# Where the zero fill of the output stands in the queue: a pooled attention with a noisy top-2 mixture of experts

## The chip, the cores and the metric

The kernel runs on one core of a Trainium2 chip. The metric is the device time of one execution in microseconds (us); lower is better. The engines that matter here are TensorE (PE in the profile, with PEld for its weight loads), VectorE (DVE), ScalarE (ACT), GpSimd (POOL), and SyncE (SP), which in this kernel does nothing but issue DMA transfers. DMA transfers issued by SP go through one hardware queue, those issued by POOL through one software queue.

## What is computed

Inputs are q, k and v of shape 8 x 8 x 576 x 64 (batch, heads, positions, head size). Keys and values are averaged over groups of 8 positions, so each query looks at 72 pooled keys. The attention result, rearranged to 4608 tokens of 512 numbers, goes into a mixture of 8 experts; each token takes its two best experts by noisy logits.

```
k_p, v_p = k.reshape(B,H,S/8,8,D).mean(3), v.reshape(B,H,S/8,8,D).mean(3)
attn = softmax(scale * q @ k_p^T) @ v_p                # 4608 tokens x 512
noisy = x @ w_gate + log1p(exp(x @ w_noise)) * noise
top2  = the two largest of noisy; weights = softmax over the two
out = zeros(4608, 512)
for e in 8 experts:  for both ranks k:
    rows = tokens whose rank-k expert is e
    out[rows] += weight * (relu(x[rows] @ w1[e]) @ w2[e])
```

w1 is 512 x 1024 and w2 is 1024 x 512 per expert. The output must start from zeros because rows are added to it expert by expert.

## The kernel before

**First part, attention (up to about 187 us of the profile).** The batch is taken in four pairs (`pr` 0 to 3), each pair in nine chunks of 128 tokens (`ci` 0 to 8), 36 chunks in all (27 to 35 are the last pair). A chunk consists of score matmuls (line 379 or 372), softmax exponentials on ACT (line 386), transposes of the exponentials (line 403) that ACT copies out of PSUM (tile `eT`, line 405), the value matmuls (line 416), and normalisation on DVE (line 427, tile `xr`). Finished tokens are written to the scratch tensor `x_dram` (line 437), by POOL in pairs 0 to 2 and by SP in the last pair. Queries of a later unit are transposed into `qp` (line 353) and copied by ACT to `qT` (line 355).

**Routing.** After each pair, `route` computes the two experts of its tokens and their places; 18 indirect DMAs per pair (line 614, POOL) scatter (token, weight) records to `rec_dram`. Two early reads of the records (tile `raw`, line 645, POOL) fetch expert 0's first lists: after the records of pair 1, and after those of pair 2. POOL then turns them into row numbers (line 684) and gathers the tokens (tile `xg`, line 706).

**Second part, the experts (from about 187 us).** The work is a list of 24 groups, three per expert; for expert 0 the groups have tiles 0 to 3, 4 to 6 and 7 to 9. `split` transposes the gathered tokens (line 928, tile `xp`) and splits them in a high and a low part (`xh`, `xl`, line 939); `stage1` multiplies by w1 in eight blocks `f` (line 968; PSUM tile `ph` with three buffers, emptied by ACT line 973 and DVE line 974); `stage2` multiplies by w2 (line 1072) and `finish` scatters results to the output (line 1014). Tiles 0 to 3 of expert 0 hold tokens of the output's lower half alone.

**Weights.** Each expert's weights come in eight loads of 512 KB through a staging tile `wst` with three buffers (line 463, SP) and are cast by ACT (line 484, high part) and DVE (line 485, low part). Expert 0's first three w1 loads are issued by SP when pair 3 begins, and the casts stand in ACT's and DVE's program at chunks 30 to 32.

**The zero fill.** `zt` is a cleared tile. `zero()` (line 124) writes it to 384 rows of the output (768 KB, line 128, SP); twelve of them cover the 4608 rows. `ZP` says after which chunk how many are emitted, and `issue_after` tells the scheduler behind which instruction they may stand in the order. The first six are the lower half, the last six the upper half (group `zero1`).

**Order.** A scheduler orders each engine's instructions when the program is built; on the chip each engine runs its own list strictly in that order and waits at semaphores.

Of the kernel before, what the change touches and what calls it, by code (L numbers as in the profile page):

```python
# [20 lines left out]
def kernel(  # L21
# [12 lines left out]
    nc = tc.nc  # L34
    B, H, S, D = q.shape
    NTOK, DM = out.shape
    E = moe_w_gate.shape[1]
    DF = moe_w1.shape[2]
    P = 128
# [7 lines left out]
    NP = B // 2  # L47
# [68 lines left out]
    ps2.tile([P, 512], F32, tag="s", name="s_first", bufs=2)  # L116

    ZW = 3
    ZP = {23: (21, 21, 22, 22), 24: (23, 23), 25: (24, 24), 26: (25, 25), 27: (26, 26)}
    lastx, laste, lastt = [None], [None], [None]  # L120
    zt = ap_.tile([P, DM], F32, name="zt")
    zn = [0]

    def zero(ins):
        i = zn[0]
        zn[0] += 1
        with tc.issue_after(ins):
            z = nc.sync.dma_start(out[i * ZW * P:(i + 1) * ZW * P, :].rearrange("(p r) m -> p r m", p=P),
                                  zt.unsqueeze(1).to_broadcast([P, ZW, DM]))
        if i * ZW * P >= XT0:  # L130
            tc.add_to_no_dep_group("zero1", z.ins)

# [207 lines left out]
    def qtr(u, half, hp=None):  # L340
        kind, pr, b, jp = u
        if half == 0:
            QTT[u] = ap_.tile([P, H, P], F32, tag="qT", name=f"qT{pr}_{b}_{jp}", bufs=2)
        elif kind == "R":
            return
        qT = QTT[u]
        qp = ps2.tile([P, 4, P], F32, tag="one", name=f"qp{pr}_{b}_{jp}_{half}", bufs=2)
        for i in range(4):
            if kind == "R":
                src = QR[pr][:, 2 * i:2 * i + 2]  # L350
            else:
                src = QT[b][:, half * 4 + i, 2 * jp:2 * jp + 2]
            nc.tensor.transpose(qp[:, i], src.rearrange("p a d -> p (a d)"), ident)
        with tc.high_priority(offset=HP if hp is None else hp):
            nc.scalar.copy(qT[:, half * 4:half * 4 + 4], qp)
# [94 lines left out]
    WST, wld = {}, {}  # L450
    genl = [None]

    def wload(e, i, h):
        st = wp.tile([P, DF], F32, tag="wst", name=f"wst{e}_{i}_{h}", bufs=WS)
        if i < 2:
            src = moe_w1[e].rearrange("(p c) f -> p c f", p=P)[:, 2 * i + h]
            dst = st
        else:
            r0 = (i - 2) * 4 * P + h * 2 * P
            src = moe_w2[e, r0:r0 + 2 * P, :].rearrange("(c p) f -> p c f", p=P)  # L460
            dst = st.rearrange("p (c f) -> p c f", c=2)
        with tc.issue_after(genl[0]) if (e, i, h) == (1, 2, 0) else nullcontext():
            wld[e, i, h] = nc.sync.dma_start(dst, src).ins
        WST[e, i, h] = st
# [27 lines left out]
    def drain(g):  # L492
        for _ in g:
            pass
# [227 lines left out]
    def fetch(g):  # L722
        e, t0, nt = g
        for t in range(t0, t0 + nt):
            gather(e, t)
# [12 lines left out]
    lgs = {}  # L738
    gens = []

    def advance(n, m):
        for _ in range(n):
            while gens:
                try:
                    next(gens[0])
                    break
                except StopIteration:
                    gens.pop(0)
        for _ in range(min(m, len(scq))):
            scq.pop(0)()  # L750
# [52 lines left out]
    for b in range(2, B):  # L803
        c = 9 * ((b - 2) // 2) + (0 if b % 2 == 0 else 4)
# [7 lines left out]
    for b in range(1, B):  # L812
        c = 9 * (b // 2) + (0 if b % 2 == 0 else 4)
# [29 lines left out]
    for i, (ui, u, jj) in enumerate(chunks):  # L843
# [17 lines left out]
        for o in order + ("" if "b" in order else "b") + ("" if "x" in order else "x"):  # L861
# [14 lines left out]
            elif ui + 2 < NU:  # L876
                qtr(units[ui + 2], "qr".index(o))
        for j in ZP.get(i, ()):
            zero(lx[j])
# [204 lines left out]
    def wadvance(n):  # L1084
        for _ in range(n):
            while wgens:
                try:
                    next(wgens[0])
                    break
                except StopIteration:  # L1090
                    wgens.pop(0)
# [3 lines left out]
    s0 = SP_[0]  # L1095
    fetch(groups[1])
    rt = route(NP - 1, 0, NCH, lgs[NP - 1], mone)

    def hook0(f):
        with tc.issue_after(s0[0].ins), tc.issue_after(s0[1].ins):  # L1100
            if f < 2:
                next(rt, None)
                next(rt, None)
            elif f == 2:
                next(rt, None)
            elif f == 5:
                drain(rt)
                advance(0, 100)
            if f < 4:
                with tc.issue_after(evict[0].ins), tc.issue_after(evict[1].ins):  # L1110
                    wadvance(2)
        if f == 4:
            for i, h in ((0, 0), (0, 1), (1, 0)):
                with tc.issue_after(wld[0, 3, 1]):
                    wload(1, i, h)
# [23 lines left out]
    for i, g in enumerate(groups):  # L1139
        e = g[0]  # L1140
        if i % NG == 1 and e + 1 < E:
            wgens += [weights(e + 1, 0), weights(e + 1, 1)]
        stage1(g, (hook0, hook2)[i] if i < 2 else None)
        if i:
            if i == 2:
                with tc.issue_after(hli[g, 2].ins):
                    split(groups[i + 1])
            elif i > 2 and i + 1 < len(groups):
                split(groups[i + 1])
            if i % NG != 1:  # L1150
                wadvance(100)
        if i % NG == NG - 1 and e + 1 < E:
            wgens += [weights(e + 1, 2), weights(e + 1, 3)]
        stage2(g, (lambda: fetch(groups[i + 2])) if 1 < i < len(groups) - 2 else (lambda: None),
               hook if i == 0 else hook1 if i == 1 else hookw if i % NG == NG - 1 else None)
        if i == 1:
            fetch(groups[3])
        if i == 0:
            lates.append(load_recs(0, E, 0, 4))
            fetch(groups[2])  # L1160
            with tc.issue_after(hli[g, NFB - 1].ins):
                wadvance(100)
# [113 lines left out]
```

## Time and profile before

| | us |
|---|---|
| median of 3 timed runs | 1045.96 (1044.1 to 1049.59) |
| span of the profiled execution, first to last instruction | 1040.8 |
| median of the timed runs minus that span | 5.16 |
| PE busy in the span | 1011.7 (97%) |
| DVE / ACT / POOL busy | 561.2 / 339.5 / 636.6 |

The profile gives the profiled execution's time as its span alone; the last line but two is what lies around it if that execution was like the median run. Times in the rows below count from the first instruction of the span. "Busy" leaves out waits and the issuing of DMAs; a row of the timeline shows in brackets how long the engine stood idle before it and what ended the wait.

### The profile page before, as it was taken

What the parts mean: (1) busy time and instruction counts of PE and PEld (TensorE: products, weight loads), DVE (VectorE), ACT (ScalarE), POOL (GpSimd) and SP (SyncE); (2) the same over time, 40 slices, a digit from 0 to 9 for tenths busy, and PEclk for the clock granted to TensorE, in tenths of its full rate; (3) what the DMA queues carried; (4) which work ended last, traced back from release to release, by engine and by line L of the source; (5) the groups of instructions that cost most, each with busy time, mean ns of one, the idle gap of its engine ahead of it and who ended that gap; (6) DMA issues with size and microseconds to landing.
All of it is one profiled execution on the core that took longest, in us unless ns stands there. A gap on an engine that the chain in (4) does not pass through costs nothing. (4 is left out here: it accounts for less than half of the span.)

```text
span 1040.8 us, 16075 instructions
## 1 busy us (share of the span) xinstructions
PE 1011.7 (97%) x5896; PEld 913.7 (88%) x5896; DVE 561.2 (54%) x1288; ACT 339.5 (33%) x857; POOL 636.6 (61%) x662
## 2 busy tenths in 40 slices
PE   7999996999999999999999999999999999999997
PEld 6999895789998998899889988998899889988995
DVE  6899884833464545444644464446445544564331
ACT  5778885512222222122222222222222222222110
POOL 4005373573776777767767776777577756773541
PEclk9999998999999999999999999999999999999998
DMA  9998996614234423442344234424432443232200
GB/s 330 365 345 246 300 314 191 160 48 115 91 91 132 140 64 104 138 134 69 117 129 140 66 113 129 130 79 118 120 124 86 114 122 117 82 91 87 69 20 32
DMA packets 77028, 142.13 MB, mean 137 GB/s; under 512 B 24501, under 2 KB 32778, under 8 KB 76948
## 3 DMA queue, kind: packets, MB, share of 16 engines
q1 hardware_dynamic: 48628, 78.33, 24.8%
q0 software_dynamic: 28320, 62.77, 19.9%
q8 instruction: 47, 0.77, 0.3%
q14 instruction: 33, 0.27, 0.1%
HBM read 103.78 MB, written 39.17 MB: 137 GB/s over the span
## 5 line engine op out<-in xcount | busy, mean ns | idle before, releaser
L968 PE MATMUL ph<-xh,w 128*128 128x384 f32 (+2 forms) x1536 | 403.9, 344 | 0.7 <-ACT xh L939 0.7
L714 POOL DMA_INDIRECT xg<-x_dram,x x266 | 261.4, 983 | 91.7 <-issue 68.3
L968 PEld LDWEIGHTS ph<-xh,w 128*128 128x128 f32 x1536 | 274.5, 188 | 21.1 <-ACT xh L939 0.9
L973 ACT ACTIVATE hh<-ph 128x512 fp32r<-128x512 f32 (+2 forms) x192 | 97.8, 509 | 548.5 <-PE ph L968 547.8
L1072 PE MATMUL py<-w,hh 128*128 128x512 f32 x896 | 276.5, 390 | 0.0
L968 PE MATMUL ph<-xl,w 128*128 128x320 f32 (+2 forms) x768 | 263.7, 344 | 0.0
L974 DVE SCALAR_TENSOR_TENSOR hl<-ph,hh 128x512 fp32r<-128x512 f32 (+2 forms) x192 | 111.3, 580 | 221.2 <-ACT hh L973 221.1
L1072 PEld LDWEIGHTS py<-w,hh 128*128 128x128 f32 x896 | 167.7, 188 | 34.3
L1072 PE MATMUL py<-w,hl 128*128 128x512 f32 x448 | 174.5, 390 | 0.0
L968 PEld LDWEIGHTS ph<-xl,w 128*128 128x128 f32 x768 | 144.2, 188 | 10.3
L1010 DVE SCALAR_TENSOR_TENSOR pv<-py,raw,pv 128x128 f32<-128x128 f32 x196 | 54.9, 342 | 130.9 <-PE py L1072 125.7
L1043 PE MATMUL py<-hh,w 128*128 128x320 f32 x512 | 112.8, 309 | 0.0
L1057 POOL DMA_INDIRECT out_dram<-pv,o x80 | 84.8, 1060 | 36.1 <-issue 13.7
L1072 PEld LDWEIGHTS py<-w,hl 128*128 128x128 f32 x448 | 84.1, 188 | 17.6
L1031 POOL DMA_INDIRECT pv<-out_dram,o x70 | 72.9, 1041 | 37.8 <-DMA out_dram<-pv,raw 18.6
L1014 POOL DMA_INDIRECT out_dram<-pv,raw x56 | 59.7, 1066 | 59.1 <-DVE pv L1010 32.0
L614 POOL DMA_INDIRECT rec_dram<-rec,pos x72 | 74.8, 1039 | 30.0 <-issue 20.1
L485 DVE TENSOR_TENSOR w<-wst,w 128x512 fp32r<-128x512 f32 x128 | 87.6, 688 | 9.7 <-ACT w L484 9.1
L1043 PEld LDWEIGHTS py<-hh,w 128*128 128x128 f32 x512 | 85.6, 188 | 0.0
L484 ACT CAST w<-wst 128x512 fp32r<-128x512 f32 x128 | 77.3, 615 | 15.2 <-DMA wst<-in_moe_w_dram 12.3
L1043 PE MATMUL py<-hl,w 128*128 128x320 f32 x256 | 79.1, 309 | 0.0
L934 DVE STREAM_TRANSPOSE xt<-xg 128x512 f32<-128x512 f32 (+1 forms) x70 | 70.9, 1035 | 3.2 <-DMA xg<-x_dram,x 2.2
(157 smaller groups left out, 982.4 us busy)
## 6 DMA issues: line engine op xcount, KB each, us to landing
wst<-in_moe_w_dram SPq DMA_DIRECT2D x64, 512.0 KB, 3.6
v<-in_v_dram SPq DMA_DIRECT2D x23, 512.0 KB, 9.2
out_dram<-zt SPq DMA_DIRECT2D x12, 768.0 KB, 19.7
k<-in_k_dram SPq DMA_DIRECT2D x7, 1280.0 KB, 11.6
q<-in_q_dram SPq DMA_DIRECT2D x7, 1024.0 KB, 12.9
x_dram<-xr POOLq DMA_DIRECT2D x12, 512.0 KB, 8.1
xg<-x_dram,x POOLq DMA_INDIRECT x276, 2.6
x_dram<-xr SPq DMA_DIRECT2D x4, 512.0 KB, 14.0
```

The lines of the kernel that those rows point to most:

```text
L484: nc.scalar.copy(hv, sv)
L485: nc.vector.tensor_sub(lv, sv, hv.bitcast(F32))
L614: s = nc.gpsimd.indirect_dma_start(out=rec_dram[:, :], out_offset=bass.IndirectOffsetOnAxis(ap=pos[:, i, c:c + 1], axis=0), in_=rec[:, c, ...
L714: nc.gpsimd.indirect_dma_start(out=xg[:, r * P:(r + 1) * P], out_offset=None, in_=x4, in_offset=bass.IndirectOffsetOnAxis(ap=xi[e, t][:, r ...
L934: nc.vector.transpose(xt[:, :nr], xg[:, :nr * P].rearrange("p (r i b) -> p r b i", i=32, b=NDB))
L968: nc.tensor.matmul(ph[:, :n], w1s(e, a, db, f), xs[b][:, db, :n], start=(i == 0), stop=(i == 3 * NDB - 1))
L973: ra = nc.scalar.activation(hh[:, :n], ph[:, :n], AF.Relu)
L974: rd = hli[grp, f] = nc.vector.scalar_tensor_tensor(hl[:, :n], ph[:, :n], 0.0, hh[:, :n].bitcast(F32), op0=OP.max, op1=OP.subtract)
L1031: g = nc.gpsimd.indirect_dma_start(out=pv4[:, i], out_offset=None, in_=out4, in_offset=bass.IndirectOffsetOnAxis(ap=oi4[e, t0 + i // 4][:, ...
L1043: nc.tensor.matmul(py[:, :n], w2s(e, b, f)[:, mb * P:(mb + 1) * P], hs[f][a][:, :n], start=(i == 0), stop=(i == 3 * NFB - 1))
L1057: s = nc.gpsimd.indirect_dma_start(out=out4, out_offset=bass.IndirectOffsetOnAxis(ap=oi4[e, t0 + i // 4][:, i % 4], axis=0), in_=r4[:, i], ...
L1072: lastm[0] = nc.tensor.matmul(py, hs[f][a][:, cs], w2s(e, b, f), start=(i == 0), stop=(i == 3 * NFB - 1))
```

## The change

The twelve zero transfers are placed otherwise. The lower six stay with `zt` as their source and move from chunks 23 to 27 to chunks 28 to 33, one each. The upper six move to the second part: they are emitted at block `f == 4` of the first group's `stage1`, to stand behind expert 0's last w2 load (`wld[0, 3, 1]`) and ahead of expert 1's first three w1 loads. Their source is no longer `zt`, whose memory is given to other tiles by then, but the logits tile of the last pair, whose first 512 columns are cleared by a new DVE memset at block `f == 2`.

```
-    ZP = {23: (21, 21, 22, 22), 24: (23, 23), 25: (24, 24), 26: (25, 25), 27: (26, 26)}
+    ZP = {28: (27,), 29: (28,), 30: (29,), 31: (30,), 32: (31,), 33: (32,)}
...
-    def zero(ins):
+    def zero(ins, src=None):
...
-                                  zt.unsqueeze(1).to_broadcast([P, ZW, DM]))
+                                  (zt if src is None else src).unsqueeze(1).to_broadcast([P, ZW, DM]))
...
     rt = route(NP - 1, 0, NCH, lgs[NP - 1], mone)
+    zrow = lgs[NP - 1].rearrange("p n h c -> p (n h c)")[:, :DM]
...
     def hook0(f):
...
+        if f == 2:
+            nc.vector.memset(zrow, 0.0)
         if f == 4:
+            while zn[0] * ZW * P < NTOK:
+                zero(wld[0, 3, 1], zrow)
             for i, h in ((0, 0), (0, 1), (1, 0)):
                 with tc.issue_after(wld[0, 3, 1]):
                     wload(1, i, h)
```

SP's list in the last quarter of the attention, before: `zt` rows are zero transfers, `wst_0_0`, `wst_0_1` and `wst_1_0` are expert 0's first three w1 loads (512 KB each), `q` the last query load, `xr` rows the tokens of pair 3.

```order
L274 DMA qr_1550<-in_q_dram 64x8x64
L128 DMA out_dram<-zt 384x1x512 x4
L269 DMA q_1899<-in_q_dram 128x8x256
L128 DMA out_dram<-zt 384x1x512 x8
L463 DMA wst_0_0_2195<-in_moe_w_dram 128x1024
L463 DMA wst_0_1_2197<-in_moe_w_dram 128x1024
L463 DMA wst_1_0_2199<-in_moe_w_dram 128x1024
L437 DMA x_dram<-xr_6_0_0_2166 128x1024
```

The same place of SP's list in the changed kernel:

```order
L274 DMA qr_1550<-in_q_dram 64x8x64
L463 DMA wst_0_0_2183<-in_moe_w_dram 128x1024
L463 DMA wst_0_1_2185<-in_moe_w_dram 128x1024
L463 DMA wst_1_0_2187<-in_moe_w_dram 128x1024
L128 DMA out_dram<-zt 384x1x512 x2
L269 DMA q_1899<-in_q_dram 128x8x256
L128 DMA out_dram<-zt 384x1x512 x4
L437 DMA x_dram<-xr_6_0_0_2156 128x1024
```

The three w1 loads have moved from behind twelve zero transfers to ahead of all; six zero transfers are left, two ahead of the query load and four behind it.

SP's list where the second part begins, before: `wst_3_0` and `wst_3_1` are expert 0's last two w2 loads, the later `wst_0_0`, `wst_0_1` and `wst_1_0` expert 1's first w1 loads.

```order
L463 DMA wst_3_0_2838<-in_moe_w_dram 128x2x512
L437 DMA x_dram<-xr_7_1_0_2638 128x1024
L463 DMA wst_3_1_2861<-in_moe_w_dram 128x2x512
L463 DMA wst_0_0_2884<-in_moe_w_dram 128x1024
L463 DMA wst_0_1_2886<-in_moe_w_dram 128x1024
L463 DMA wst_1_0_2888<-in_moe_w_dram 128x1024
```

The same place in the changed kernel:

```order
L463 DMA wst_3_0_2832<-in_moe_w_dram 128x2x512
L437 DMA x_dram<-xr_7_1_0_2632 128x1024
L463 DMA wst_3_1_2856<-in_moe_w_dram 128x2x512
L128 DMA out_dram<-lg_2110 384x1x512 x6
L463 DMA wst_0_0_2885<-in_moe_w_dram 128x1024
L463 DMA wst_0_1_2887<-in_moe_w_dram 128x1024
L463 DMA wst_1_0_2889<-in_moe_w_dram 128x1024
```

Six zero transfers with the cleared logits as their source now stand between expert 0's last load and expert 1's first.

## Rows read from the trace of the kernel before

**Rows 1.** The page: span of the profiled execution.
```profile
span 1040.8 us, 16075 instructions
```
**Rows 2.** Windows: stretch, length, busy us (instructions) per engine, PE clock, DMA share, GB/s.
```profile
165.00:170.00 5.00, 1.68 (x8) 1.57 (x8) 2.40 (x5) 2.43 (x5) 0.58 (x1) 0.50 0.29 88
...
190.00:1000.00 810.00, 809.97 (x4299) 729.75 (x4300) 398.23 (x823) 197.24 (x385) 548.64 (x545) 1.00 0.35 105
```
**Rows 3.** Timeline, 166 to 173 us: start, duration, engine, line, what, [idle before <-releaser].
```profile
166.37 1.14 ACT L484 CAST w<-wst 128x512 fp32r<-128x512 f32 x2 [11.28 <-DMA wst<-in_moe_w_dram]
...
168.32 1.97 PE L353 MATMUL qp<-ident,q 128*128 128x128 f32 x8 [9.36 <-ACT eT L405]
...
172.61 0.43 PE L403 MATMUL ep<-ident,ex 128*112 128x128 f32 x2
```
**Rows 4.** Timeline of SP's DMA issues: start, time to issue them.
```profile
104.28 6.56 SPq L128 DMA_DIRECT2D out_dram<-zt  x4
...
119.27 27.33 SPq L128 DMA_DIRECT2D out_dram<-zt  x8
146.65 6.64 SPq L463 DMA_DIRECT2D wst<-in_moe_w_dram  x3
...
198.13 8.32 SPq L463 DMA_DIRECT2D wst<-in_moe_w_dram  x4
```
**Rows 5.** Tile `wst`, loads issued from 146 to 158 us.
```profile
DMA to landing us min/median/max: 16.8/18.3/19.7
```
**Rows 6.** Timeline of PE, the same kind of chunk one pair earlier.
```profile
117.78 1.04 PE L353 MATMUL qp<-ident,q 128*128 128x128 f32 x8
...
120.28 0.32 PE L403 MATMUL ep<-ident,ex 128*112 128x128 f32 x1
```
**Rows 7.** Tile `zt`: its memset (ns min/median/max), and its twelve transfers.
```profile
L185 POOL MEMSET zt<- x1: 565/565/565, 8.8 to 8.8; 128x512 f32 x1
...
DMA to landing us min/median/max: 13.8/19.7/21.7
```
**Rows 8.** Timeline of POOL: records, the two early reads, gathers.
```profile
155.53 1.02 POOL L614 DMA_INDIRECT rec_dram<-rec,pos  x1 [0.30 <-issue]
165.60 0.58 POOL L645 DMA_DIRECT2D raw<-rec_dram  x1 [9.04 <-DMA rec_dram<-rec,pos]
...
175.02 0.95 POOL L706 DMA_INDIRECT xg<-x_dram,x  x1 [0.31 <-issue]
...
198.65 0.97 POOL L614 DMA_INDIRECT rec_dram<-rec,pos  x1 [0.30 <-issue]
204.59 0.59 POOL L645 DMA_DIRECT2D raw<-rec_dram  x1 [4.97 <-DMA rec_dram<-rec,pos]
...
212.04 0.94 POOL L706 DMA_INDIRECT xg<-x_dram,x  x1 [0.30 <-issue]
```
**Rows 9.** Landings: `rec` issued 130 to 158 us; `rec` 212 to 236; `xg` 165 to 180.
```profile
DMA to landing us min/median/max: 7.5/9.9/10.7
...
DMA to landing us min/median/max: 2.2/2.9/4.3
...
DMA to landing us min/median/max: 3.4/6.1/8.9
```
**Rows 10.** Timeline of PE: transposes of expert 0's gathered tokens.
```profile
187.22 2.10 PE L928 MATMUL xp<-ident,xg 128*128 128x128 f32 x16
...
228.67 1.12 PE L928 MATMUL xp<-ident,xg 128*128 128x128 f32 x8
```
**Rows 11.** Tile `wst`, loads issued from 197 to 207 us.
```profile
DMA to landing us min/median/max: 6.0/6.0/6.0
```
**Rows 12.** Timeline, 206 to 241 us: an eviction, block 7 of stage 1, expert 1's first cast.
```profile
206.01 0.68 DVE L974 SCALAR_TENSOR_TENSOR hl<-ph,hh 128x512 fp32r<-128x512 f32 x1
...
209.40 0.62 PE L968 MATMUL ph<-xh,w 128*128 128x512 f32 x2
...
240.43 0.61 ACT L484 CAST w<-wst 128x512 fp32r<-128x512 f32 x1
```

## The prediction, made before the changed kernel ran

> **What bounds the kernel now.** I read four views, in this order. The windows come first. From 190 to 1000 us PE is busy 809.97 of 810.00 us [rows 2], so the second part is PE from end to end: it takes up no slack, and any microsecond won or lost ahead of it goes straight into the end. The reader is to see that DVE and POOL are far from full there. What this change can touch lies before 190 us, and the one large hole there is in the timeline: PE stood idle 9.36 us before the query transposes at 168.32, released by ACT's copy to `eT` [rows 3]. ACT had not been busy either: it stood 11.28 us before its cast at 166.37, and what ended that was the landing of a `wst` load. The cast is of a weight that is first used after the transposes of 187.22 [rows 10], but it stands ahead of the `eT` copies in ACT's list, and ACT takes its list in order.
>
> The third view, SP's issues, says why that load was late. The three w1 loads were issued from 146.65, behind twelve zero transfers issued from 104.28 to 146.60 [rows 4]. They needed 16.8 to 19.7 us to land [rows 5]; the first, 146.65 + 19.7 = 166.3, is the release that ACT saw. Loads issued near 198 us, with no zeros about, needed 6.0 us [rows 11]. So the loads queued behind the zeros. The fourth view, POOL's timeline, is for what comes due next, and is used below.
>
> **The change part by part.** *The w1 loads ahead of the zeros.* They take the slots from 104.28 on, where four zero transfers were: three loads and two zeros are 3 x 512 + 2 x 768 = 3072 KB, four zeros are 4 x 768 = 3072 KB. The query load at about 118.8 therefore has the same bytes ahead of it as before, and nothing before 119 us changes. Even with the zeros' longest landing, 21.7 us [rows 7], loads issued by about 108 are there by 130, 25 us before ACT wants the first. The whole wait of ACT goes, and with it PE's: **-9.36 us**.
>
> *The restart.* After the hole PE's granted clock was 0.50 from 165 to 170 us [rows 2], that is 1.2 GHz, the lower of its two levels. From the query transposes to the first `ep` transposes it took 172.61 - 168.32 = 4.29 us [rows 3]; the same 8 transposes and 24 value matmuls one pair earlier took 120.28 - 117.78 = 2.50 us [rows 6]. Without the hole the stretch should run as the earlier one: **-1.79 us**. Bounds are 0 and that; I take the full value, since the stretch is the same work. What is late behind it I keep as it is: the gaps after 172 us end at `eT` copies that follow PE's own work.
>
> *The lower zeros.* Four stay behind the query load, where eight were. Nothing waits for them soon: the first scatter to the output comes behind group 0's second stage, which starts after the transposes of 187.22 [rows 10] and the whole first stage. They cost nothing, and the queue is clear earlier by six transfers, which is what lets the record scatters land sooner (below).
>
> *The memset.* One 128 x 512 clear; the only such row is POOL's, 0.565 us [rows 7]. DVE's can be put between 0 and 0.57. It stands in DVE's list ahead of block 0's eviction, and `ph` has three buffers. The tightest place that I priced: block 4's eviction ends at 206.01 + 0.68 = 206.69, and block 7, which takes its buffer, starts at 209.40, 2.71 us later [rows 12]. The memset fits: 0.
>
> *The upper zeros.* SP issues them behind the load of 198.13, which will be at 198.13 - 11.15 = 187.0. Eight transfers took SP 27.33 us with the queue full [rows 4], so six take at most 20.5, and expert 1's first load goes out by 207.5 and lands by 227.2 with the 19.7 of [rows 5]. ACT's first cast of it is at 240.43 - 11.15 = 229.3 [rows 12]: 0, with 2 us to spare in the worst case.
>
> *What comes due sooner.* Two POOL chains have to move up too. First: the early read was issued at 165.60, when the last record scatter of 155.53 had landed after 10.1 us. Record scatters land in 7.5 to 10.7 us under the zeros and in 2.2 to 4.3 in a quiet queue [rows 9]. With the four zeros gone by then I take 4.3: read at 159.8, 5.8 us sooner. The last gather of group 0 moves from 175.02 to 169.2 [rows 8] and lands at the median of 6.1 us [rows 9] at 175.3, at the longest, 8.9, at 178.1. PE wants that fourth tile three quarters into the transposes of 187.22 to 189.32 [rows 10], at 188.8 - 11.15 = 177.6. Price 0, at most 0.5.
>
> Second: group 1. Its last record scatter goes out at 198.65 - 5.8 = 192.9, now under the upper zeros; with 10.7 us it lands at 203.6. From the read to the last gather it is 212.04 - 204.59 = 7.45 us [rows 8], so 211.0, and landed at 217.1 (median) or 219.9 (longest). PE's transposes are at 228.67 - 11.15 = 217.5 [rows 10]. Price 0, at most 2.4.
>
> **Sum.** -9.36 - 1.79 = -11.15 us on the profiled span of 1040.8 us [rows 1]: 1029.65. The median of the timed runs is 5.16 above that span, so I forecast 1045.96 - 11.15 = **1034.8 us**.
>
> **A rule that speaks against it.** The record scatters issued from 130 to 158 us landed in at most 10.7 us [rows 9] while zero transfers took up to 21.7 [rows 7], so the row says that POOL's small transfers get through beside SP's large ones. The Trainium skill, "DMA: Bandwidth & Descriptors", section "Queues, rings and completion order", says that a transfer's completion signal lands only after every earlier write of that DMA engine, across its queues. Read strictly, a record scatter would not count as landed until the zero writes begun before it are done; the trace shows only part of that. By the rule the second chain is late, and that is rival B below, with its time worked out from the rows alone.
>
> **The rivals.** *A, the early read keeps its time.* If the record scatters' 10.1 us is not the zeros' doing, the read stays at 165.60, the last gather of group 0 at 175.02, landed at 183.9 at the longest, and PE, wanting it at 177.6, waits 6.3 us. The gain is then 4.9: 1041.1. For it: POOL's own 512 KB token write stands ahead of the last scatter. Against it: quiet scatters take 4.3 at most.
>
> *B, the second chain waits for the upper zeros.* They are issued at 187.0; if the scatters' landing waits for the last of them, 21.7 us, the read goes out at 208.7, the last gather at 216.2, landed at 222.3, and PE waits 222.3 - 217.5 = 4.8 us: 1039.6. For it: six transfers at once, just as the scatters are issued. Against: the 10.7 us above.
>
> *C, slower: the last w2 load shares the queue with the six zeros behind it.* Before, three loads stood behind it; now 4.6 MB do, with no wait between. If transfers of one queue share the engines instead of following each other, it lands not in 6.0 us but in something like the 19.7 of a load among zeros, 13.7 later. ACT's cast of it stands ahead of the evictions, which have 2.71 us to spare, so PE would wait 11.0 us and restart at the lower clock for another 1.8: 12.8 lost against 11.15 won, 1047.6. It eats the whole gain from a landing of 6.0 + 2.71 + 9.36 = 18.1 us on. Against it: in [rows 5] the loads were late by what stood ahead of them, and the load of 198.13 did not suffer from those behind.
>
> *D, it does not do what it says.* Some other late transfer takes the place of the w1 load at 159 us and PE waits as long: 1046. I see no candidate; key, value and query loads have the same bytes ahead.
>
> **How the numbers follow.** Forecast 0.72, A 0.09, B 0.10, C 0.05, D 0.04. What a measurement of this kernel can tell from no change is 0.5%, or 5.2 us, so the line for faster is 1040.7. Faster: the forecast, B, and half of A, which lies on the line: 0.72 + 0.10 + 0.04 = 0.86. Same: the rest of A, D and a third of C: 0.10. Slower by over 0.5%, above 1051.2, needs C with a landing beyond 23 us: 0.04. The range starts 3.3 below the forecast (the fastest run is 1.9 below the median, and of the small gaps before 187 us one or two more may close) and goes up to A: 1031.5 to 1041.0. The likeliest case's own range is 1032 to 1038, with the bounds of 0.5 and 2.4 and the restart.
>
> **What will show it.** Right: SP issues three `wst` loads at about 104; ACT's first cast follows at about 155 without a wait; no PE hole and no granted clock of 0.50 between 159 and 175; group 0's transposes at about 176; PE without a gap through the upper zeros. The early read at about 160 confirms the first chain; at 165 it is A. A wait of `xp` for `xg` near 217 is B; a wait of ACT's cast for `wst` near 193 and a PE hole near 198 is C. The forecast is wrong if group 0's transposes start later than 181, or if PE is idle over 3 us in 176 to 300.

## The result, and the profile after

The changed kernel takes 1038.50 us, the median of 7 runs (1034.84 to 1043.09); before, run beside it, takes 1048.11 us (7 runs, 1044.10 to 1051.55). The ratio is 0.9906, with a 95% interval of 0.9883 to 0.9929: faster by 9.9 us, with bounds of 7.4 and 12.3. I had forecast 1034.8 us and 11.15 us of gain, so the sign and the range are right and the gain is a little smaller than forecast. A second set of runs of the same kernel (below) gave 0.9929 (0.9895 to 0.9962). Some versions below were run on two chips where before itself took 1287 and 1289 us at a granted clock of about 0.90; none of them was faster than before there (1.0036 to 1.0197) and those times decide nothing below, so the gain is shown only for chips where before runs at 0.98 to 0.99.

The profiled execution of after took 1040.2 us, 2.1 more than its span, and its span is only 2.7 us below that of [rows 1]:

```profile
span 1038.1 us, 16083 instructions
```

So the two profiles differ by less than the timed runs do. The windows say why. First after, then before, both with the columns of [rows 2] (the last but two is PE's granted clock, 1.00 being 2.4 GHz and 0.50 being 1.2 GHz):

```profile
26.00:52.00 26.00, 25.59 (x189) 23.52 (x188) 18.90 (x39) 15.11 (x52) 2.03 (x3) 0.74 1.03 363
159.00:175.00 16.00, 15.47 (x137) 14.07 (x137) 12.50 (x43) 13.54 (x46) 7.06 (x10) 1.00 0.46 146
...
300.00:400.00 100.00, 97.31 (x519) 87.98 (x519) 51.02 (x99) 26.25 (x51) 72.33 (x73) 1.00 0.36 109
```
```profile
26.00:52.00 26.00, 25.39 (x228) 23.66 (x227) 22.67 (x48) 19.40 (x68) 2.03 (x3) 0.95 1.04 365
159.00:175.00 16.00, 6.33 (x48) 5.49 (x48) 4.02 (x10) 6.29 (x22) 3.82 (x5) 0.68 0.55 183
300.00:400.00 100.00, 100.00 (x533) 90.50 (x533) 53.39 (x108) 27.36 (x53) 73.09 (x73) 1.00 0.37 110
```

The reader is to see three things. In 26 to 52 us, where the two programs do the same, after got a clock of 0.74 where before got 0.95, and did 189 matmuls instead of 228: a start that this one execution had, not the change. In 159 to 175 the hole is gone: 15.47 us busy of 16 at full clock, where before had 6.33 at 0.68. And in 300 to 400, where before had no idle time, after has 2.69 us of it, which I had not forecast.

The slow start can be taken out. The query transposes of [rows 6] stood at 117.78 and are at 122.77 now, 4.99 us later; earlier ones were 5.00 us later already at 44.54 (39.54 in before), long before anything that the change touches. Below, "on the clock of before" means a time of after less 4.99. This is the timeline of after, SP, ACT and PE, to be held against [rows 3, 4, 6, 10]:

```profile
109.79 2.40 SPq L463 DMA_DIRECT2D wst<-in_moe_w_dram  x3
...
122.77 1.04 PE L353 MATMUL qp<-ident,q 128*128 128x128 f32 x8
...
158.49 1.28 PE L353 MATMUL qp<-ident,q 128*128 128x128 f32 x8
...
160.39 1.13 ACT L484 CAST w<-wst 128x512 fp32r<-128x512 f32 x2
...
164.20 1.04 PE L353 MATMUL qp<-ident,q 128*128 128x128 f32 x8
...
166.70 0.44 PE L403 MATMUL ep<-ident,ex 128*112 128x128 f32 x2
...
181.46 2.11 PE L928 MATMUL xp<-ident,xg 128*128 128x128 f32 x16
...
222.91 1.12 PE L928 MATMUL xp<-ident,xg 128*128 128x128 f32 x8
```

The w1 loads go out at 104.8 on the clock of before, ACT's cast has no wait behind its name, and from the query transposes to the first `ep` it takes 166.70 - 164.20 = 2.50 us, where before took 4.29. Group 0's transposes are at 181.46 - 4.99 = 176.47, which is 10.75 us sooner than in [rows 10]. In before, the last query transposes ahead of the hole are these:

```profile
153.08 1.28 PE L353 MATMUL qp<-ident,q 128*128 128x128 f32 x8
```

From them to group 0's transposes it takes 187.22 - 153.08 = 34.14 us in before and 181.46 - 158.49 = 22.97 in after. So the hole and the restart, forecast at 11.15, are worth 11.17; 0.42 us was lost ahead of them, between the transposes of 122.77 and those of 158.49 (35.72 us, against 35.30 in before).

POOL's two chains, against [rows 8]:

```profile
164.89 0.59 POOL L645 DMA_DIRECT2D raw<-rec_dram  x1 [3.75 <-DMA rec_dram<-rec,pos]
...
173.63 0.95 POOL L706 DMA_INDIRECT xg<-x_dram,x  x1 [0.30 <-issue]
...
197.78 1.33 POOL L614 DMA_INDIRECT rec_dram<-rec,pos  x1 [0.30 <-issue]
207.01 0.59 POOL L645 DMA_DIRECT2D raw<-rec_dram  x1 [7.90 <-DMA rec_dram<-rec,pos]
...
215.78 0.95 POOL L706 DMA_INDIRECT xg<-x_dram,x  x1 [0.30 <-issue]
```

The first read comes at 159.90 on the clock of before, 5.7 us sooner; the second, with the upper zeros beside it, at 202.02, only 2.6 sooner, since it waits 7.90 us instead of 4.97. PE's waits in after, and then the place of the longest of them, with the rows of SP, POOL and DVE that lead to it:

```profile
PE ph L968 <- DVE hl L974: 2.7, 1, 2.7
...
PE qp L353 <- ACT eT L405: 1.3, 3, 0.5
```
```profile
353.94 0.38 SPq L463 DMA_DIRECT2D wst<-in_moe_w_dram  x1
...
355.12 1.02 POOL L1014 DMA_INDIRECT out_dram<-pv,raw  x1 [0.30 <-DVE xl L939]
360.32 1.01 POOL L1031 DMA_INDIRECT pv<-out_dram,o  x1 [4.18 <-DMA out_dram<-pv,raw]
...
372.04 1.11 POOL L1031 DMA_INDIRECT pv<-out_dram,o  x1 [0.30 <-issue]
...
374.29 0.35 DVE L1054 SCALAR_TENSOR_TENSOR pv<-yt,w,pv 128x128 f32<-128x128 f32 x1 [1.05 <-DMA pv<-out_dram,o]
374.56 1.01 DVE L974 SCALAR_TENSOR_TENSOR hl<-ph,hh 128x384 fp32r<-128x384 f32 x2
...
375.16 0.44 PE L968 MATMUL ph<-xh,w 128*128 128x384 f32 x1 [2.69 <-DVE hl L974]
```

The same place before:

```profile
357.82 1.01 POOL L1014 DMA_INDIRECT out_dram<-pv,raw  x1 [0.30 <-issue]
361.45 1.01 POOL L1031 DMA_INDIRECT pv<-out_dram,o  x1 [2.62 <-DMA out_dram<-pv,raw]
...
373.16 0.99 POOL L1031 DMA_INDIRECT pv<-out_dram,o  x1 [0.30 <-issue]
...
375.29 0.35 DVE L1054 SCALAR_TENSOR_TENSOR pv<-yt,w,pv 128x128 f32<-128x128 f32 x1 [0.23 <-DMA pv<-out_dram,o]
```

From the bottom up: PE waits for an eviction `hl`. In DVE's list that stands behind ten additions L1054 of expert 1's small group, and these wait for ten reads L1031 of old output rows, which POOL issues 1.30 us apart and not before expert 1's first output scatters L1014 have landed. In before, DVE waited 0.23 us for the last of them; in after it waited for six. The first matmuls L1043 of expert 1 start at 357.74 in before and at 351.99 in after: the reads began 3.7 us behind them in before and 8.3 us behind them in after. On the clock of before the last addition moved from 375.29 to 369.30, by 6.0 us, while PE moved by 10.7. The reads were just in time, and now they are late. That costs 2.98 us: from the first L1043 of expert 1 to that of expert 2 it takes 459.65 - 351.99 = 107.66 us, against 104.68 in before.

The account of the two profiles: -11.17 for hole and restart, +0.42 ahead of them, +2.98 at 375 us and +4.99 for the slow start make -2.78; the spans differ by 2.7. Without the slow start the change is worth 7.8 us by this trace, inside the interval. The changed kernel's second profile, further down, gives another account.

### The profile page after: what moved, and what is told of

The parts are those of the page before. It is cut to its first block, busy times and chain, and to the rows that moved or that the text cites. A ratio compares the mean times of both kernels' runs of the same rounds, so it can differ in the third digit from the quotient of the medians.

```text
span 1038.1 us, 16083 instructions
## 1 busy us (share of the span) xinstructions
PE 1015.6 (98%) x5896; PEld 917.2 (88%) x5896; DVE 561.3 (54%) x1289; ACT 339.5 (33%) x857; POOL 636.0 (61%) x662
## 5 line engine op out<-in xcount | busy, mean ns | idle before, releaser
L1043 PE MATMUL py<-hh,w 128*128 128x320 f32 x512 | 112.8, 309 | 0.0
L1031 POOL DMA_INDIRECT pv<-out_dram,o x70 | 73.7, 1053 | 39.4 <-DMA out_dram<-pv,raw 20.2
L1014 POOL DMA_INDIRECT out_dram<-pv,raw x56 | 58.6, 1047 | 51.1 <-DVE pv L1010 31.7
L1043 PEld LDWEIGHTS py<-hh,w 128*128 128x128 f32 x512 | 85.6, 188 | 0.0
L1043 PE MATMUL py<-hl,w 128*128 128x320 f32 x256 | 79.1, 309 | 0.0
```

The costliest lines, as they stand in the source:

```text
L1031: g = nc.gpsimd.indirect_dma_start(out=pv4[:, i], out_offset=None, in_=out4, in_offset=bass.IndirectOffsetOnAxis(ap=oi4[e, t0 + i // 4][:, ...
L1043: nc.tensor.matmul(py[:, :n], w2s(e, b, f)[:, mb * P:(mb + 1) * P], hs[f][a][:, :n], start=(i == 0), stop=(i == 3 * NFB - 1))
```

## The experiments

Theory P: GpSimd's own chain (table scatters, table read, row gathers, output scatters, row reads) is the second pacemaker. The zeros held it back, the hole had hidden that, and PE meets it at 375 us. The rivals stand in each expectation.

**The order alone, without zeros in the expert part.** All twelve zeros behind the w1 loads, the memset and the upper zeros of the expert part taken out:

```diff
-    ZP = {28: (27,), 29: (28,), 30: (29,), 31: (30,), 32: (31,), 33: (32,)}
+    ZP = {28: (27, 27), 29: (28, 28), 30: (29, 29), 31: (30, 30), 32: (31, 31), 33: (32, 32)}
```

> All twelve zero transfers follow expert 0's first w1 loads in the attention part, out of the zero tile; none is issued in the expert part. Theory P (GpSimd's chain of row scatters, table reads and row gathers is the second pacemaker behind TensorE): ScalarE's cast at about 155 us waits under 1 us, so the hole of before is gone, but twelve zeros now run beside the first half's table scatters as they did before the change. The first table read then comes at about 165 us instead of 160 (counted on the clock of before), group 0's transposes lose about 3 to 5 us of the 10.8 gained, and the kernel takes 1041 to 1044 us where the changed one takes 1038.5. Rival Q (only the order of the zeros and the w1 loads counts, and GpSimd's reads have room): the same as the changed kernel within 1 us, 1037.5 to 1039.5, and without the 2.7 us wait of TensorE at 375 us, since no zeros run beside the second table read.

Measured: 1307.87 us, 1.0197 of before, on one of the chips at 0.90. So again:

> The kernel of e1_all_behind once more (in that call every kernel, before too, ran at a mean granted clock near 0.90 and took about 1290 us). All twelve zeros behind expert 0's first w1 loads in the attention part, none in the expert part. Theory P (GpSimd's chain is the second pacemaker): no hole at ScalarE's cast, but the first table read waits 6 to 9 us and comes at 165 to 166 us on the clock of before; group 0's transposes lose 2 to 5 us of the 10.8 gained; the second read waits only 4 to 5 us, so GpSimd stands where it stood before the change and the wait of TensorE at 375 us is 2 to 4 us. 1040 to 1044 us, 0.993 to 0.998 of before. Rival Q (only the order of zeros and w1 loads counts): 1035 to 1039, 0.988 to 0.991, no wait at 375.

Measured: 1044.73 us, 0.9967 (0.9942 to 0.9991). The ratio is where P had put it, and above rival Q's range. Theory P holds in its first half: the hole is gone, but the first read waits as in [rows 8], and PE waits three times for gathered rows and runs at a clock of 0.72 there. The rows are a wait row, a POOL row and two windows of this kernel:

```profile
PE xp L928 <- DMA xg<-x_dram,x: 6.2, 3, 2.3
```
```profile
173.25 0.58 POOL L645 DMA_DIRECT2D raw<-rec_dram  x1 [10.16 <-DMA rec_dram<-rec,pos]
```
```profile
300.00:400.00 100.00, 100.00 (x544) 91.27 (x543) 51.89 (x103) 27.34 (x53) 73.00 (x74) 1.00 0.39 109
176.00:200.00 24.00, 16.23 (x71) 12.83 (x71) 13.92 (x36) 8.26 (x20) 16.60 (x18) 0.72 0.46 144
```

Its second half failed: I had expected a wait at 375 us, and there is none. PE had been held up at 183 us already, and POOL's row reads began 3.6 us behind expert 1's first L1043, as in before. This is what rival A of the prediction would have looked like, and it shows what the upper half costs in the attention part, even behind the w1 loads.

**The upper half moved alone.** The lower six zeros stay ahead of the w1 loads:

```diff
-    ZP = {28: (27,), 29: (28,), 30: (29,), 31: (30,), 32: (31,), 33: (32,)}
+    ZP = {23: (21, 21, 22, 22), 24: (23, 23)}
```

> The lower six zeros keep their old place ahead of the w1 loads; the upper six go behind the last w2 load, as in the changed kernel. Theory P: the w1 loads are issued behind six zeros instead of twelve, at about 125 to 130 us, land 17 to 20 us later, at 142 to 150, and the cast at about 155 waits under 1 us; so the moved upper half alone removes the hole, the second table read waits 7 to 8 us as in the changed kernel, TensorE waits 2 to 4 us at about 375 and the time is that of the changed kernel, 1036.5 to 1040.5. Rival R (the loads must be ahead of every zero): the cast waits 4 to 6 us, about half of the 9.4 of before, and the time is 1042 to 1044.

Measured: 1288.66 us, 1.0036, at a clock of 0.907. Again:

> The kernel of e2_upper_out once more, for the same reason. The lower six zeros at their old place ahead of the w1 loads, the upper six behind the last w2 load. Theory P: the w1 loads are issued at about 125 to 130 us behind six zeros instead of twelve and land by 150, the cast at about 155 waits under 1 us, the second table read waits 7 to 9 us as in the changed kernel, TensorE waits 2 to 4 us at about 375: the time of the changed kernel, 0.989 to 0.993 of before. Rival R (the loads must be ahead of every zero): the cast waits 4 to 6 us and the time is 0.994 to 0.997.

Measured: 1041.29 us, 0.9942 (0.9919 to 0.9965). SP issued the w1 loads at 129.31, they landed in at most 15.4 us, and ACT did not wait: rival R is out by its mechanism. The time does not decide: 0.9942 is 0.001 above what P gave and at the lower end of R's range, and it can't be told from the second set of the changed kernel, whose interval overlaps. The profiled execution was the fastest of its 13 runs, 1030.27 us, 11 us below their median. It had neither the slow start nor the wait:

```profile
26.00:52.00 26.00, 25.09 (x236) 23.44 (x235) 23.68 (x50) 20.08 (x69) 2.02 (x3) 1.00 1.04 365
159.00:175.00 16.00, 14.55 (x115) 12.64 (x112) 11.02 (x28) 13.58 (x47) 11.06 (x12) 1.00 0.71 179
300.00:400.00 100.00, 100.00 (x533) 90.50 (x532) 51.90 (x103) 25.14 (x49) 73.66 (x75) 1.00 0.38 112
```
```profile
span 1028.3 us, 16079 instructions
```

That is 12.5 us below [rows 1]; my sum had been 1029.65. Its second read waited 8.28 us, as long as in the changed kernel, and yet PE did not wait at 375: the row reads began 3.6 us behind expert 1's first L1043. So a long second read does not always lead to the wait. Whether the edit kept POOL in time, or chance in this one execution, is not shown; the changed kernel waited in both of its profiles.

**The changed kernel again.**

> The changed kernel itself, once more beside the next one, so that both stand against the same runs of before. Theory P (GpSimd's chain is the second pacemaker): 0.988 to 0.993 of before, at a mean granted clock near 0.99 about 1036 to 1040 us; ScalarE's cast at about 160 us without a wait, the second table read after a wait of 7 to 8 us, and a wait of TensorE for DVE's hl of 2 to 3.5 us at about 375 us. Rival U (that wait belongs to the one profiled execution): no wait over 1 us there.

Measured: 1041.42 us, 0.9929 (0.9895 to 0.9962). Rival U is out: the wait is there again, 2.36 us, and this time the granted clock falls behind it, so that the stretch from expert 1's to expert 2's L1043 takes 460.95 - 352.07 = 108.88 us instead of 104.68, 4.20 more:

```profile
374.91 0.64 PE L968 MATMUL ph<-xh,w 128*128 128x384 f32 x1 [2.36 <-DVE hl L974]
```
```profile
370.00:380.00 10.00, 7.64 (x35) 7.32 (x34) 3.95 (x10) 2.49 (x5) 7.56 (x9) 0.83 0.14 34
```

This execution had no slow start (1.00 at 26 to 52 us), and its span of 1039.4 us is still only 1.4 below that of [rows 1]. The rows say where the gain went:

```profile
117.49 1.04 PE L353 MATMUL qp<-ident,q 128*128 128x128 f32 x8
...
126.58 0.46 PE L403 MATMUL ep<-ident,ex 128*112 128x128 f32 x1 [3.68 <-ACT ex L386]
157.82 1.28 PE L353 MATMUL qp<-ident,q 128*128 128x128 f32 x8
...
180.78 2.11 PE L928 MATMUL xp<-ident,xg 128*128 128x128 f32 x16
```
```profile
124.97 0.69 DVE L427 TENSOR_TENSOR xr<-a,rd 128x512 f32<-128x512 f32 x1 [4.21 <-DMA x_dram<-xr]
```

Hole and restart are worth 34.14 - 22.96 = 11.18 us here too. But from the transposes of 117.49 to those of 157.82 it takes 40.33 us where before took 35.30. PE waited 3.68 us (1.23 at this place in before), at the end of a chain that starts with DVE waiting 4.21 us (1.77 in before) until a token write to `x_dram` had landed; behind that wait the granted clock was 0.84 from 117 to 130 us and 0.95 from 130 to 159, where before had 1.00. With 0.29 us won ahead of it and 0.77 lost between the transposes of group 0 and expert 1's L1043, this account is -0.29 + 5.03 - 11.18 + 0.77 + 4.20 = -1.47. The same stretch took 35.0 and 35.3 us in the two profiles with four zeros behind the load of `qr` (the upper half moved alone, and before), and 35.7 to 40.3 in the five with the w1 loads and two zeros there. So the changed order may itself cost 0.4 to 5 us at this place. No run was made to tell that from chance, and this stays open.

**The upper zeros later.** They leave the second half's table scatters and go behind the tile table's read:

```diff
-            while zn[0] * ZW * P < NTOK:
-                zero(wld[0, 3, 1], zrow)
...
+        if t == 3:
+            nc.vector.memset(zrow, 0.0)
+            while zn[0] * ZW * P < NTOK:
+                zero(wld[1, 1, 0], zrow)
```

> The lower six zeros as in the changed kernel; the upper six are issued behind expert 1's first three w1 loads and behind the tile table's read, at about 212 to 219 us instead of 193, so that they no longer run beside the second half's table scatters. Theory P: the second table read waits 4 to 5 us instead of 7.9, all of GpSimd's chain comes 3 to 3.7 us sooner, the 2.7 us wait of TensorE at 375 us goes, and the time falls by 2 to 3 us from 1038.5, to 1035.5 to 1036.5 (0.988 of before). Rival S (the wait at 375 us comes from the transfers of that place and not from GpSimd's lateness since 207 us): the wait stays at 2 to 3 us and the time at 1038 to 1039. Rival T (the zeros now slow group 1's row gathers or the last table scatters by as much): a TensorE wait at 218 to 225 us, or the same wait at 375, and 1038 to 1041.

Measured: 1297.51 us, 1.0117, at a clock of 0.905. The edit did not do what it was meant to: the zeros came out at 286 us only, behind the output scatters that stand ahead of them in the program. Mended (cleared behind tile 1, and declared apart from the scatters to the other half of the rows):

> The run e3_upper_late mended: there the upper six zeros stood in the program behind the first output scatters and waited for them, until 286 us, and held the last table read behind them. Here they are declared apart from those rows and their source is cleared behind group 0's second tile, so they are issued at about 213 to 220 us (in the changed kernel at 193 to 198). Theory P: the second table read waits 4 to 5 us instead of 7.9, all of GpSimd's chain from there on comes 3 to 3.7 us sooner, the wait of TensorE at 375 us shrinks from 2.7 to under 0.5 us, and the time is 2 to 3 us below the changed kernel's. Rival S (the wait at 375 us does not come from the second read): the read is sooner, the wait and the time stay within 1 us of the changed kernel's. Rival T (the zeros now slow the row gathers or the third part's table scatters by as much): the time within 1 us of the changed kernel's or up to 3 us above, with a wait of TensorE at 218 to 225 us or the same wait at 375.

Measured: 1033.30 us (6 runs, 1031.25 to 1040.86), 0.9877 (0.9845 to 0.9909), beside the second set of the changed kernel, whose interval overlaps this one. In its one profile the wait at 375 is gone; a window, and the POOL rows that decide:

```profile
300.00:400.00 100.00, 100.00 (x534) 90.48 (x532) 51.16 (x99) 26.24 (x51) 73.83 (x74) 1.00 0.37 113
```
```profile
353.50 1.02 POOL L1014 DMA_INDIRECT out_dram<-pv,raw  x1 [0.30 <-issue]
356.90 1.01 POOL L1031 DMA_INDIRECT pv<-out_dram,o  x1 [2.38 <-DMA out_dram<-pv,raw]
```

The reads start 3.4 us sooner than in after, though PE is 1.15 us later there: 3.8 us behind expert 1's first L1043. P expects that, but its route was only half right. The second read did wait less, 5.61 us, yet other scatters stalled for 2.27 us and the read was no sooner against PE than in after. What helped more seems to lie behind it: the program's order changed with the edit, and three of group 0's output scatters, 1.3 us each, came to stand ahead of the last table read's first use, inside POOL's wait for it (6.79 us in after, 3.38 here). Two changes were made at once, so I tried to part them:

> The changed kernel with its zeros where they are, but GpSimd's order as in e6_upper_behind_t1: group 0's second to fourth output scatters stand ahead of the first use of the last table read (and not between and behind group 2's row gathers). e6 had moved both, the zeros and this order. Theory P1 (what helped in e6 is that three scatters of 1.3 us, 3.9 us in all, fill GpSimd's wait for the last table read): the second table read still waits 7 to 9 us, the wait for the last table read falls from 6.8 or 5.7 us to 2 to 3, TensorE's wait at 375 us falls from 2.7 or 2.4 to under 0.5, the stretch from expert 0's to expert 1's last-group products from 107.6 or 108.8 us to 104.7, and the time is that of e6, 0.985 to 0.989 of before. Theory P2 (the zeros beside the second half's table scatters are what costs): the wait stays at 2 to 3 us, the stretch at 107 to 109 and the time at 0.990 to 0.993.

> The kernel of e6_upper_behind_t1 once more, beside e7_order_alone. Theory P1 and P2 both: no wait over 0.5 us of TensorE at 375 us, 104.7 us for the stretch from expert 0's to expert 1's last-group products, 0.985 to 0.990 of before. By P1 e7_order_alone equals it within 1 us, by P2 it is 2 to 4 us below e7_order_alone. If its first result was chance, it lies at 0.990 to 0.993.

Measured: 1295.62 us, 1.0102, and 1299.89 us, 1.0079, both on a chip at 0.90. How much of the mended kernel's gain is the zeros' place and how much the order is not settled.

**POOL four microseconds later.** The opposite test: eight memsets on POOL in the changed kernel, behind group 1's gathers.

```diff
...
+    junk = mp.tile([P, 400], F32, name="junk")
+    with tc.issue_after(lg1[6]):
+        for _ in range(8):
+            lj[0] = nc.gpsimd.memset(junk, 0.0)
```

> The changed kernel with eight memsets of 128x400 on GpSimd, about 4 us, between group 1's row gathers and the third part's table scatters (at about 217 us). Theory P: GpSimd has no room left between there and the reads of the old rows that end at 372 us, so these reads and the wait of TensorE at 375 us become later by the same 4 us: a wait of 6 to 7 us there and 1042 to 1043 us in all. Rival Q (GpSimd has room of 4 us or more before TensorE asks): the wait stays under 3.5 us and the time at 1038 to 1039.

Measured: 1294.60 us, 1.0103, at a clock of 0.916. Again:

> The kernel of e5_pool_plus4 once more, for the same reason: the changed kernel with eight memsets of 128x400 on GpSimd, about 4 us, between group 1's row gathers and the third part's table scatters. Theory P: the wait of TensorE at 375 us grows from 2.4 or 2.7 us to 6 to 7, and the time by 3.5 to 5 us over the changed kernel's: 1041 to 1045, 0.994 to 0.998 of before. Rival Q (GpSimd has room of 4 us or more): the wait stays under 3.5 us and the time at 0.989 to 0.993.

Measured: 1050.71 us, 1.0032 (1.0009 to 1.0056): no faster than before, and outside what either P or Q gave. The wait at 375 grew to 3.79 us; P had given 6 to 7, Q less than 3.5. The row reads began 9.5 us behind expert 1's first L1043, only 1.2 to 1.6 later than in the two profiles of the changed kernel, since PE had itself waited 1.2 us for POOL at 252 us and part of the delay was taken up in between. The stretch from expert 1's to expert 2's L1043 took 465.04 - 353.35 = 111.69 us, with a clock that fell behind the wait as in the changed kernel's second profile; with the 1.2 us at 252 that is 4.0 to 5.2 us more than in the two profiles of the changed kernel, for 4 us put in. So POOL does not have the 4 us of room that Q needs, but the wait did not grow as P said. And the whole is some 10 us slower, more than P allows. Much of the rest lies after 600 us, where the same PE, always busy and at full clock, did 2071 matmuls in 400 us instead of 2109; this window of the experiment, then of after:

```profile
600.00:1000.00 400.00, 400.00 (x2071) 354.68 (x2070) 193.06 (x380) 96.09 (x186) 262.78 (x260) 1.00 0.35 103
```
```profile
600.00:1000.00 400.00, 400.00 (x2109) 359.59 (x2108) 191.90 (x386) 92.50 (x179) 260.23 (x258) 1.00 0.34 101
```

Whether that comes from the extra tile or from POOL's lateness was to be told by a version without the tile:

> As e5_again, but the eight memsets (128x384, about 4 us in all) on GpSimd write into a tile that is there already and is overwritten later, so that no tile lies elsewhere in memory. In e5_again the stretch from expert 0's to expert 1's last-group products took 111.6 us (107.6 and 108.8 in the changed kernel's two profiles), and matmuls of 128x512 at 620 to 740 us stood 0.233 us apart instead of 0.227, which cost another 4 us or so. Theory P (GpSimd has no room; the slow matmuls came from the extra tile's place): 111 to 113 us for the stretch, matmuls 0.227 apart, 0.993 to 0.997 of before. Rival V (the slow matmuls come from GpSimd's lateness too): 1.001 to 1.005 again. Rival Q (GpSimd has room): 0.990 to 0.993.

Measured: 1293.56 us, 1.0067, at a clock of 0.91: the time gives no answer. The traces do. Take the neighbouring starts of stage 1's matmuls that lie 0.21 to 0.25 us apart. With the tile, 65% of them are 0.231 to 0.236 us apart in the kernel that took 1050.71 us, and 59% in its first run, at a clock of 0.916; without the tile, with the same eight memsets, it is 7%, as in the other kernels on such chips (7 to 8%), and 1 to 2% in the other kernels elsewhere. The slow matmuls go with the tile, so rival V is out; why a tile does that is not shown. (The expectations of the three last runs name the stretch of L1043 by the wrong experts; it is from expert 1's to expert 2's.)

## Why the prediction was right, and what it missed

- **The w1 loads ahead of the zeros, -9.36: right.** Issued at 104.8 on the clock of before, landed in 16.2 to 18.6 us, and no wait of ACT. The experiment with the upper half moved alone shows more than I had claimed: six zeros ahead of the loads bring no wait of ACT, twelve do. What I had not priced is the stretch from 118 to 158 us behind the new order: 0.42 us lost in one profile of the changed kernel and 5.03 in the other.
- **The restart, -1.79: right.** The stretch took 2.50 us as in [rows 6]. Together the two gave 11.17 and 11.18 us in the two profiles, for a forecast of 11.15.
- **Lower zeros, memset: right at 0.** No idle time of PE in 176 to 300 us comes near the 3 us that I had set as the mark of a failure, and none of its waits there is for `hl`.
- **The last w2 load with the zeros behind it: right at 0.** It landed in 5.4 us, and ACT waited 0.39 us for it; rival C's 13.7 us more did not come.
- **The first chain, price 0: right.** Read at 159.90 (forecast 159.8), last gather at 168.64 (169.2), transposes at 176.47 (176.07).
- **The second chain, "Price 0, at most 2.4": right where I priced it, wrong as a step.** The read came at 202.02 (at most 203.6), the last gather at 210.79 (211.0), and group 1's transposes at 217.92 (217.5) without a wait for it; rival B did not happen. The six zeros were issued from 192.79 to 197.58 and landed 8.9 to 15.4 us later (row below), the last at 212.97, while the scatter of 197.78, issued behind them, counted as landed by 207.01. The rule of the Trainium skill that I had weighed ("DMA: Bandwidth & Descriptors", section "Queues, rings and completion order") speaks of earlier writes of a DMA engine. The row tells when transfers were issued, not when each engine wrote, so it does not decide on the rule. But I closed the account at 217.5. My own numbers said that PE would come 11 us sooner and the second read 1 us sooner, so POOL had lost 10 us against PE, and I asked only whether the next tile was there. In before, POOL still had a pause of 8.36 us at 259 us, where it waited for DVE; in after that pause is gone, used up (rows below), and from there to the row reads of 360 to 373 us POOL was late. There the debt fell due: 2.98 us in one profile, 4.20 in the other. The pause stood in POOL's timeline of before, but I had stopped reading at 240. That it is the six zeros beside the second record scatters that make POOL late is not shown: with them in the same place, the upper half moved alone had no wait in its profile, and the version that moved them moved POOL's order too.
The landing of those six zeros, tile `lg` of after (us, least, median, longest):

```profile
DMA to landing us min/median/max: 8.9/14.1/15.4
```
POOL's pause in before, and the same scatter in after:

```profile
259.36 0.98 POOL L1014 DMA_INDIRECT out_dram<-pv,raw  x1 [8.36 <-DVE pv L1013]
```
```profile
257.07 0.98 POOL L1014 DMA_INDIRECT out_dram<-pv,raw  x1 [0.30 <-issue]
```

- **The sum.** -11.15 became -7.8 in the first trace, without its slow start, and -1.4 in the second; the two ratios give -9.9 and -7.4. The forecast of 1034.8 stood on a median of 1045.96 that came out as 1048.11 with more runs. The 5.16 us between span and median were no constant part either: in after's runs 2.1 to 2.2 us lie around the span. By that the profiled execution of before took about 1042.9 us, less than any of its timed runs, so both traces of the changed kernel are held against an execution of before that took less time than its timed ones. The mechanism was worth 11.2 us, as forecast, and costs that I had put at nothing took 1.3 and 3.7 us of it back in the timed runs. The first set's median lies in the range that I gave; the second's, 1041.42, is 0.4 above its end.

## What to carry to other kernels

When a hole on the busiest engine closes, every other engine keeps its own pace: write down by how much each chain moves up, and follow the one that moves least to the next place where the busy engine needs it, however far that is, not only to the next tile. Zeros, and other transfers that nobody waits for, cost where they run beside small transfers that somebody does wait for. A profile of one execution can be several us off at a place where two programs do the same; take that out before the spans are compared, and profile the changed kernel twice: here the two profiles lost the gain at different places.

## What the runs showed of the hardware

The granted clock of the same instructions at 26 to 52 us was 0.95, 0.74 and 1.00 in three executions (before, after and the upper half moved alone), with 228, 189 and 236 matmuls done. In after PE stood 4.99 us behind before at the query transposes that followed. The timed runs of after go with their mean clock: 1034.84 and 1035.74 us at 0.998 and 0.999, the five others, 1036.53 to 1043.09, at 0.991 to 0.996.

How long a row scatter took to land went with whether a 512 KB load was issued ahead of it. In after the scatter of 355.12 was issued 1.2 us behind a load of 353.94, and the read that waits for it started 5.20 us later; in before, where the load (359.70) came 1.9 us behind the scatter, it took 361.45 - 357.82 = 3.63 us, and in the mended kernel with the later zeros, with the load at 355.10, 356.90 - 353.50 = 3.40 us. The four other profiles at a clock near 1.00 fall in the same two groups: 4.83 us (the changed kernel again) and 5.17 (POOL four microseconds later) behind the load, 3.26 (the upper half moved alone) and 3.51 (the order alone) ahead of it. No run moved the load by itself. If the load is the cause, 1.6 to 1.8 of after's 2.69 us come from the scatter falling behind it, and the rest from POOL's lateness.
